# Attention into a gated MoE layer on one core: first batch loaded in fp32 with long rows and cast on the engines, weights behind it, output phase one block late, first MoE tiles by chunk

## The chip, the core and the metric

The kernel runs on one core of a Trainium2 chip. The metric is device microseconds (us) of one execution, of which several are taken. One of the four executions of the kernel before took 997.29 us against 419.54 to 422.00 for the others; it is left out of every ratio (the median of four below still counts it; without it the median is 421.95).

## The reference, cut to what matters

Eight batches of linear attention (8 heads, 576 tokens, head size 64) with a normalised output, then a gated layer over all 4608 tokens of width 512, with 1536 hidden features. Inputs and outputs are fp32.

```python
kv  = einsum('bhsd,bhse->bhde', k, v)          # q, k, v: (8, 8, 576, 64)
o   = einsum('bhsd,bhde->bhse', q, kv)
x   = o / sqrt(mean(o*o, axis=-1) + 1e-6) * g_norm
x   = x.transpose(0, 2, 1, 3).reshape(4608, 512)
ffn = (gelu(x @ w_gate) * (x @ w_val)) @ w_out  # 512 -> 1536 -> 512
out = x + sigmoid(x @ w_res) * ffn
```

## The kernel before

The tokens are cut in blocks of 512: the first 512 tokens of each batch are blocks 0 to 7, and the 64 left over in each batch together make block 8. A block of the MoE layer has 16 slots: twelve feature tiles (eight matmuls of 512 columns each: a gate product `gps` and a value product `vps`) and four output tiles (sixteen matmuls each: `rps`, `fps`). The attention of the next batch is woven into those slots by a fixed plan. Tiles lie in SBUF, the core's memory, here over 128 partitions (its rows) or fewer; results of matmuls lie in the banks of PSUM. Matmuls run on fp16 copies; the DMA that brings in a batch casts it on the way.

```python
    def load_batch(b):                      # (cut: tiles, tokens 512 to 575, q of the rest)
        for j, src in enumerate(main_rows(q, b)):     # rows of 64 fp32 = 256 B
            nc.gpsimd.dma_start(out=q_sb[:, j, :].rearrange("p (h d) -> p h d", h=H), in_=src)
        # ... the same for k and v, four DMAs each, then the rests of k, v and q

    load_batch(0)
    ident32 = consts.tile([P, P], FP32, name="ident32")
    make_identity(nc, ident32)              # POOL: behind the issues of load_batch(0)
    # ... mask, g (broadcast by a DMA to all partitions)
    load_weights()                          # 14 DMAs: gate, value, residual, output
    load_batch(1)                           # behind all weights in the same queue
    # ...
    # one plan of the attention of batch b by slot of the block before it:
    #  0,1: q transposes   2: kv   4-7: outputs   9: norm, scaling   10-15: scalings, transposes of x
    plan = attn_slots(0)                    # batch 0: alone, ahead of block 0
    for s in range(16):
        for f in plan[s]:
            f()
    for blk in range(B + 1):
        # ... load_batch(blk + 2)
        plan = attn_slots(blk + 1)
        for s in range(16):
            if s < NF:
                m_gval(blk, s)              # feature tile s of this block
            else:
                m_out(blk, s - NF)          # output tile of the same block
            for f in plan.get(s, []):
                f()
```

## Time and profile before

| what | value |
|---|---|
| time, median of 4 runs | 421.98 us |
| TensorE busy, of the profiled span of 422.0 us | 358.7 us, 85% |
| packets of the software queue (casting DMAs) | 120928 |
| first MoE matmul | 44.3 us |
| start of block 1 | 105.9 us |
| a block from there on | 39.8 (even batch woven in) or 40.4 us (odd) |

The profile names engines: PE is TensorE (PEld its weight loads), DVE VectorE, ACT ScalarE, POOL GpSimd, SP the engine that issues the plain DMAs. A row of 40 digits gives the busy share of one fortieth of the span in tenths. A line of the order of time has start, duration, engine, source line, operation, what it writes and reads, shapes, and in brackets the idle time ahead of it with what ended it. In a table by stretch, the granted clock is the share of the full TensorE clock that the profile records as granted. Half and full clock, or cold and warm, are names here for two paces of TensorE in the traces: four matmuls of 512 columns took 1.86 to 1.91 us (44.32 and 56.72 in the kernel before) or 1.03 (from 60.12), and a matmul of 128 columns 0.107 or 0.056.

### The profile page before, as it was taken

What the parts mean: (1) busy time and instruction counts of PE and PEld (TensorE: products, weight loads), DVE (VectorE), ACT (ScalarE), POOL (GpSimd) and SP (SyncE); (2) the same over time, 40 slices, a digit from 0 to 9 for tenths busy, and PEclk for the clock granted to TensorE, in tenths of its full rate; (3) what the DMA queues carried; (4) which work ended last, traced back from release to release, by engine and by line L of the source; (5) the groups of instructions that cost most, each with busy time, mean ns of one, the idle gap of its engine ahead of it and who ended that gap; (6) DMA issues with size and microseconds to landing.
All of it is one profiled execution on the core that took longest, in us unless ns stands there. A gap on an engine that the chain in (4) does not pass through costs nothing.

```text
span 422.0 us, 5322 instructions
## 1 busy us (share of the span) xinstructions
PE 358.7 (85%) x2048; PEld 179.5 (43%) x2048; DVE 213.0 (50%) x411; ACT 161.1 (38%) x277; POOL 112.2 (27%) x140
## 2 busy tenths in 40 slices
PE   0052457979998999899899989998999899999994
PEld 0041124524544555445445544554455444444441
DVE  1028111775468447744764586457446853334432
ACT  1024122713463266345434652472347333312320
POOL 6396369940560074009201900000000000000000
PEclk9999998989999999999999999999999999999999
DMA  0999999992790199019911951100200020011013
GB/s 16 100 164 195 207 157 129 142 89 75 68 126 10 66 103 92 26 75 100 69 51 50 137 34 51 50 2 0 75 27 2 0 76 25 1 51 50 0 27 75
DMA packets 127242, 29.45 MB, mean 70 GB/s; under 512 B 114416, under 2 KB 122608, under 8 KB 127216
## 3 DMA queue, kind: packets, MB, share of 16 engines
q0 software_dynamic: 120928, 19.41, 61.5%
q1 hardware_dynamic: 6288, 9.70, 6.7%
q8 instruction: 16, 0.26, 0.3%
q14 instruction: 10, 0.08, 0.1%
HBM read 39.06 MB, written 9.44 MB: 115 GB/s over the span
## 4 chain that ended last, share of the span: by engine, by line
PE 73%; DMA 12%; DVE 8%; POOL 3%; issue 1%; ACT 1%; DVEq 0%; POOLq 0%
PE fps L321 22%; PE gps L299 18%; PE vps L304 18%; PE rps L316 7%; DMA wo<-in_moe_w_out_dram 4%; DMA q_sb<-in_q_dram 4%; PE xtp L264 2%; DMA wv<-in_moe_w_val_dram 2%; POOL v_sb L90 2%; DMA vr<-in_v_dram 2%; PE kvp L174 2%; PE op L193 1%; PE qtp L165 1%; DVE t L250 1%; DVE hid L309 1%
## 5 line engine op out<-in xcount | busy, mean ns | idle before, releaser
L309 DVE TENSOR_TENSOR hid<-ge,vps 128x512 f16<-128x512 f16 x108 | 74.2, 687 | 82.0 <-PE vps L304 81.7
L299 PE MATMUL gps<-xT,wg 128*128 128x512 f16 x432 | 113.1, 385 | 0.7 <-ACT xT L265 0.7
L304 PE MATMUL vps<-xT,wv 128*128 128x512 f16 x432 | 112.1, 382 | 0.0
L321 PE MATMUL fps<-wo,hid 128*128 128x512 f16 x432 | 100.5, 383 | 0.0
L308 ACT ACTIVATE ge<-gps 128x512 f16<-128x512 f32 x108 | 64.8, 600 | 84.0 <-PE gps L299 80.6
L321 PEld LDWEIGHTS <-hid 128*128 128x128 f16 x432 | 42.7, 99 | 52.2 <-issue 2.4
L304 PEld LDWEIGHTS <-wv 128*128 128x128 f16 x432 | 42.6, 99 | 52.3 <-issue 2.3
L86 POOL DMA_DIRECT2D q_sb<-in_q_dram x32 | 28.4, 913 | 108.6 <-PE qtp L165 104.0
L299 PEld LDWEIGHTS <-wg 128*128 128x128 f16 x432 | 40.3, 99 | 38.1 <-issue 2.5
L326 DVE SCALAR_TENSOR_TENSOR pf<-th,fps 128x512 f32<-128x512 f32 x36 | 24.8, 689 | 60.2 <-PE fps L321 60.2
L265 ACT COPY xT<-xtp 128x512 f16<-128x512 f16 x36 | 21.1, 586 | 78.1 <-PE xtp L264 78.1
L165 PE MATMUL qtp<-ident,q_sb 128*128 128x128 f16 x128 | 11.0, 236 | 32.4 <-DVE ident L112 24.6
L316 PE MATMUL rps<-wr,xT 128*128 128x512 f16 x144 | 37.3, 382 | 0.0
L186 DVE TENSOR_REDUCE ss<-sq 128x8 f32<-128x512 f32 x36 | 24.7, 686 | 21.9 <-ACT sq L185 21.9
L166 ACT COPY qT<-qtp 128x1024 f16<-128x1024 f16 x16 | 16.1, 1012 | 43.0 <-PE qtp L165 43.0
L324 ACT ACTIVATE th<-rps 128x512 f32<-128x512 f32 x36 | 21.5, 598 | 27.5 <-PE rps L316 27.5
L90 POOL DMA_DIRECT2D v_sb<-in_v_dram x32 | 28.6, 956 | 9.5 <-DMA q_sb<-in_q_dram 9.5
L88 POOL DMA_DIRECT2D k_sb<-in_k_dram x32 | 28.4, 934 | 9.3 <-DMA wo<-in_moe_w_out_dram 6.2
L264 PE MATMUL xtp<-ident,x 128*128 128x128 f16 x144 | 14.9, 229 | 17.4 <-DVE x L256 17.4
L328 DVE SCALAR_TENSOR_TENSOR osb<-pf,x 128x512 f32<-128x512 f32 x36 | 24.9, 692 | 1.2
L250 DVE TENSOR_TENSOR t<-o,ny 128x512 f16<-128x512 f32 x36 | 24.7, 686 | 0.3
L165 PEld LDWEIGHTS <-q_sb 128*128 128x128 f16 x128 | 9.3, 105 | 36.5 <-DMA q_sb<-in_q_dram 26.7
(49 smaller groups left out, 211.3 us busy)
## 6 DMA issues: line engine op xcount, KB each, us to landing
out_dram<-osb SPq DMA_DIRECT2D x32, 256.0 KB, 2.0
q_sb<-in_q_dram POOLq DMA_DIRECT2D x32, 128.0 KB, 4.3
k_sb<-in_k_dram POOLq DMA_DIRECT2D x32, 128.0 KB, 4.6
v_sb<-in_v_dram POOLq DMA_DIRECT2D x32, 128.0 KB, 4.9
wg<-in_moe_w_gate_dram POOLq DMA_DIRECT2D x6, 256.0 KB, 8.0
wv<-in_moe_w_val_dram POOLq DMA_DIRECT2D x6, 256.0 KB, 8.6
wo<-in_moe_w_out_dram POOLq DMA_DIRECT2D x1, 1536.0 KB, 17.9
out_dram<-osb SPq DMA_DIRECT2D x8, 128.0 KB, 2.3
```

Source lines behind the costliest of these rows:

```text
L86: nc.gpsimd.dma_start(out=q_sb[:, j, :].rearrange("p (h d) -> p h d", h=H), in_=src)
L88: nc.gpsimd.dma_start(out=k_sb[:, j, :].rearrange("p (h d) -> p h d", h=H), in_=src)
L90: nc.gpsimd.dma_start(out=v_sb[:, j, :].rearrange("p (h d) -> p h d", h=H), in_=src)
L250: nc.vector.tensor_tensor(out=t16, in0=s["o"][j].rearrange("p (h d) -> p h d", h=H), in1=s["rinv"][:, j, :, None].to_broadcast([P, H, D]), ...
L299: nc.tensor.matmul(gps, lhsT=wg_c[wi][:, cc, wo_ : wo_ + P], rhs=xT[:, cc, :], start=(cc == 0), stop=(cc == NP - 1))
L304: nc.tensor.matmul(vps, lhsT=wv_c[wi][:, cc, wo_ : wo_ + P], rhs=xT[:, cc, :], start=(cc == 0), stop=(cc == NP - 1))
L308: nc.scalar.activation(out=ge, in_=gps, func=AF.Gelu)
L309: nc.vector.tensor_tensor(out=hids[blk][:, f, :], in0=ge, in1=vps, op=ALU.mult)
L316: nc.tensor.matmul(rps, lhsT=xT_t[blk][:, cc, js], rhs=wr16[:, cc, :], start=(cc == 0), stop=(cc == NP - 1))
L321: nc.tensor.matmul(fps, lhsT=hid[:, f, js], rhs=wo16[:, f, :], start=(f == 0), stop=(f == NF - 1))
L326: nc.vector.scalar_tensor_tensor(out=pf, in0=th, scalar=1.0, in1=fps, op0=ALU.add, op1=ALU.mult)
L328: nc.vector.scalar_tensor_tensor(out=osb, in0=pf, scalar=0.5, in1=x_t[blk][:, j, :], op0=ALU.mult, op1=ALU.add)
```

## The change

The intent is to shorten the start. Its parts:

1. **Load.** Tokens are assigned to partitions so that a partition's tokens are adjacent in memory: four tokens of q on each of 128 partitions (rows of 1024 B), six tokens of k and v on each of 96 partitions (rows of 1536 B). Batch 0 comes as fp32 on SP's queue in halves and is cast on ACT, DVE and POOL; the later batches still use POOL's casting DMA, now with long rows and a 16-bit reorder copy on DVE.
2. **Order of the loads.** The first eight weight pieces are issued by POOL behind its cast, then batch 1, then the rest of the weights.
3. **First MoE tiles by chunk.** Feature tiles 0 and 1 of block 0 are done in four token chunks of 128, so that a chunk can begin when its quarter of x is there.
4. **Output phase one block behind.** A block does its twelve feature tiles and then the four output tiles of the block before it. The last block does two output phases.
5. **Smaller things.** Batch 1's attention starts in slot 7 of block 0; batch 0's norm uses a square root on ACT; the scale by g moves into the copy of the transpose; PSUM is split four and four instead of six and two.

```diff
+    def src_q(b, lo, hi):
+        return q[b, lo:hi, 0:M0, :].rearrange("h (p j) d -> p h (j d)", j=NJ)
+    def src_kv(t, b, lo, hi):
+        return t[b, lo:hi, :, :].rearrange("h (p i) d -> p h (i d)", i=NI)
 ... cut: load_batch for b > 0, with the same rows and POOL's casting DMA ...
-    load_batch(0)
+    for lo in (0, HH):
+        nc.sync.dma_start(out=raw[0, "q"][:, lo : lo + HH, :], in_=src_q(0, lo, lo + HH))
+    for lo in (0, HH):
+        for which, t in (("k", k), ("v", v)):
+            nc.sync.dma_start(out=raw[0, which][:, lo : lo + HH, :], in_=src_kv(t, 0, lo, lo + HH))
 ... cut: identity, mask, constants ...
+    by_token_q(0, 0, HH, nc.scalar.copy)
+    by_token_q(0, HH, H, nc.scalar.copy)
+    a_qT(0, 0)
+    a_qT(0, 1)
+    by_token_k(0, 0, HH, nc.vector.tensor_copy)
+    nc.gpsimd.tensor_copy(out=b16_t[0, "v"][:, 0:HH, :], in_=raw[0, "v"][:, 0:HH, :])
+    a_kv(0, 0, 2)
+    for i in range(4):
+        load_wgv(i)
+    by_token_k(0, HH, H, nc.vector.tensor_copy)
+    nc.vector.tensor_copy(out=b16_t[0, "v"][:, HH:H, :], in_=raw[0, "v"][:, HH:H, :])
+    a_kv(0, 2, 4)
 ... cut: outputs, norm by square root and scaling, chunk by chunk ...
+    nc.vector.tensor_copy(out=grow16, in_=grow[:, None, :].to_broadcast([1, H, D]))
+    gps = pattn.tile([P, C], FP32, tag="at", name="gbp")
+    nc.tensor.matmul(gps, lhsT=ones16, rhs=grow16.rearrange("p h d -> p (h d)"), start=True, stop=True)
+    nc.vector.tensor_copy(out=g16, in_=gps)
 ...
+    def m_gval_first(blk, after):
+        for j in range(NJ):
+            after(j)
+            for f in range(2):
+                m_mm(tiles[2 * f], wg_c, f, blk, j, j + 1)
+                m_mm(tiles[2 * f + 1], wv_c, f, blk, j, j + 1)
 ...
+            first = 7 if blk == 0 else 1
+            plan = {first + i: s for i, s in enumerate(attn_plan(nxt))}
+        if blk == 0:
+            slots = [lambda: m_gval_first(0, lambda j: a_xT(0, j)), None]
+            slots += [lambda f=f: m_gval(0, f) for f in range(2, NF)]
+        else:
+            slots = [lambda f=f: m_gval(blk, f) for f in range(NF)]
+            slots += [lambda j=j: m_out(blk - 1, j) for j in range(NJ)]
+        if blk == B:
+            slots += [lambda j=j: m_out(blk, j) for j in range(NJ)]
 ...
+            if blk == 0 and s == 2:
+                load_batch(1)
+                load_wgv(4)
+                load_wgv(5)
```

## The prediction

> **What bounds the kernel now.** I read the busy slices of the page first, then the table by stretch, then the chain of waits of the start, then the order of time around each hole in TensorE.
>
> ```profile
> PE   0052457979998999899899989998999899999994
> DMA  0999999992790199019911951100200020011013
> q0 software_dynamic: 120928, 19.41, 61.5%
> ```
>
> One slice is 10.55 us. TensorE is full from about the eighth slice on; before that the DMA row is full. The queue row gives 259.5 us of 16 engines for 120928 packets, 34 ns each.
>
> By stretch (busy of PE, weight load, DVE, ACT, POOL; then clock, DMA share, GB/s):
>
> ```profile
> 0.00:44.32 44.32, 8.98 (x69) 6.91 (x69) 12.59 (x37) 9.58 (x15) 28.51 (x40) 1.00 1.22 123
> 44.32:68.60 24.28, 12.60 (x61) 6.20 (x61) 2.07 (x3) 3.72 (x5) 13.22 (x16) 0.95 1.84 164
> 106.79:146.60 39.81, 38.67 (x230) 19.47 (x229) 23.35 (x47) 17.77 (x31) 12.58 (x15) 1.00 0.77 72
> 347.50:382.30 34.80, 34.80 (x163) 15.79 (x162) 13.82 (x21) 9.72 (x17) 0.00 (x0) 1.00 0.09 31
> ```
>
> Two regimes. From 106.8 us on, a block costs 39.8 us with an even batch's attention in it and 40.4 us with an odd one's; block 7, without attention, costs 34.8. A block has 160 MoE matmuls of 512 columns, which go at 0.86 us for four in the chain, 34.5 us. So the steady part is TensorE itself. The first 106 us hold one such block and some 65 us of waiting. The chain of waits and the order of time show what for:
>
> ```profile
> 24.57 1.86 PE L165 MATMUL qtp<-ident,q_sb 128*128 128x128 f16 x16 [24.57 <-DVE ident L112]
> 44.32 1.86 PE L299 MATMUL gps<-xT,wg 128*128 128x512 f16 x4 [0.67 <-ACT xT L265]
> ```
>
> ```profile
> 36.71 17.87 DMA wo<-in_moe_w_out_dram
> 55.75 3.51 POOL v_sb L90 x4
> 59.95 6.73 DMA vr<-in_v_dram
> 68.59 1.34 PE gps L299 x4
> ```
>
> Batch 0 lands by about 27 us. Even the identity is made only at 24 us, as its POOL instructions queue behind the load. The first MoE matmul is at 44.3. Then batch 1, which stands behind all weights in the queue, holds TensorE until 68.6, because its attention is woven into block 0.
>
> [...]a batch is 13824 rows of 256 B and took some 26 us (1.25 to 27.5), 864 rows per engine, 30 ns or 8.5 GB/s per engine; the gate and value weights, rows of 1024 B, 512 per DMA, landed one every 1.34 us (POOL's starts at 38.05, 39.38, 40.75, 42.05, 43.40), 32 rows per engine, 42 ns or 24 GB/s, 390 GB/s over all. [...]The trace's two casts (128 columns 0.23 us, 512 columns 0.43) differ by 0.52 ns per element[...]; the 16-bit rate has no instance here. [...]at 84 us, with POOL issuing DMAs, three small tensor_scalar took 0.77 to 0.84 us, against 0.18 at 36 us. [...]at 44.3 and 56.7 us four matmuls took 1.86 and 1.91 us, from 60 us 1.03 or less.
>
> **The change part by part.**
>
> *Batch 0 load.* 3.4 MB in rows of 1024 B (q) and 1536 B (k, v) on the SP queue, in halves q, q, k, v, k, v, with no DMA cast. At 390 GB/s a q half (0.52 MB) is 1.35 us and a k or v half (0.59 MB) 1.5 us. SP issues its first DMA at 0.74 us; I take 2 us to landing, as the stores show. Landings: 4.1, 5.5, 7.0, 8.5, 10.0, 11.5 us. Against 27.5 before this is 16 us less.
>
> *Casts.* ACT q halves of 1024 elements, about 1.0 us each (the qT copy of 1024 takes 1.01): ready at 6.6, then transposes and qT copies, ready by 10. DVE k half of 1536: 0.16+1536x0.52 ns = 0.96 us. POOL v half: I choose 2 us (its select over 128 columns took 0.29), 10.5 us, TensorE's first half of kv then. DVE casts the second halves by 12.5. Twelve matmuls at cold pace 1.3 us, 13.9; mask 0.69, 14.7.
>
> *Rest of batch 0's attention.* Square from PSUM at 15.8 (0.6), four reductions at 0.69 to 18.6, then on DVE four times a reciprocal (0.15) and a scaling (0.69) with small gaps, 22.1. This replaces the long norm chain of 2.7 us and the eight output evictions. The gelu table load (1.28 in the trace) sits in ACT's gap.
>
> *First MoE tiles by chunk.* The instruction order shows the broadcast of g (cast on DVE behind the last scaling, then a matmul) ahead of the first transpose in TensorE's queue, so no chunk starts before about 22.7: the overlap with the scalings is lost. Then each chunk is serial: transposes 0.4, copy with pointer scale 0.7, 16 matmuls of 128 columns at 0.056 to 0.107, with hand-overs 2.5 us. Four chunks: 32.7 us for feature tiles 0 and 1. Before, they were complete only at about 59 us.
>
> *Block 0.* Ten tiles x 1.73 = 17.3 us. Weights start at 10.5 behind POOL's cast: eight DMAs x 1.35 are in at about 22; batch 1, now long rows, needs 3.4 MB / 390 = 8.7 us plus 512 short rows at 30 ns per engine-row (1 us): in by 33; the last four gate and value pieces by 39, before tile 8 at about 43. So DMA no longer ends any wait. Attention of batch 1 in block 0: 44 small matmuls x 0.056 = 2.5 us, and 0.5 of waits. The last tile ends at 53.0.
>
> *The new hole.* With the output phase a block behind, block 0 has 12 slots while batch 1's attention occupies slots 7 to 20: its outputs, norm and transposes come with nothing beside them. ACT: six passes at 0.5 us, 3.4 us after that tile; last reduction 4.2; norm 12 operations at 0.22, 6.9; four scalings 9.7; transpose and copy 10.9. Block 1 starts at 63.9, and a cold clock costs it 1.7: 65.6 us.
>
> *The remainder.* Blocks 1 to 6 took 240.7 us (39.81+40.40+39.90+40.40+39.80+40.40); 24 instead of 20 matmuls for kv add 4x0.056 each: 242.0. Blocks 7 and 8 took 68.3 (347.5 to 415.8), and block 0's output phase comes on top, 64x0.2158 = 13.8: 82.1. Tail from the last matmul to the end 6.2, as before.
>
> Sum: 65.6+242.0+82.1+6.2 = 395.9, so **396 us**, 6% less. A check: block 1 began at 105.9 before; at 65.6 with 13.8 owed it stands at 79.4, 26.5 less, minus 1.3 for kv.
>
> *PSUM and DVE in the steady part.* Tiles for MoE fall from six to four. The product of tile 10 waits behind norm and two scalings (about 4 us of DVE); its bank is wanted by the output matmuls one tile and a residual group later. The stall I find is about 1.1 us at the first transpose, and the kernel before has that same one (1.14 us idle before its transpose at 130.69, ended by DVE), so I add nothing. The two extra DVE casts per block[...] fit the slack of a tile.
>
> **The rivals.**
> 1. *A PSUM or DVE bound in steady blocks.* Against: DVE is 23 to 25 us busy of 40[...]. For: four banks leave one tile of slack[...]. 1 to 2.5 us per block for six blocks: 402 to 411.
> 2. *The hole is larger or smaller.* The norm's small operations at the 0.84 seen under POOL's issues would add 2 us; the chain starting earlier would take 3 off. 393 to 399.
> 3. *The load does not reach 390 GB/s, or POOL's cast is slow.* [...]4 us of POOL cast gives 2 more and delays the weights. 397 to 400.
> 4. *The load was hidden anyway.* Then the time would stay at 422. Against: the holes of 7.6 us at 48 to 55 and the 24.57 at the start are TensorE's own, and nothing else fills them.
> 5. *Startup quicker* (chunks at 2 us, hole 8): 388 to 391.
>
> **Range and chances.** The saving of 26 us comes from landings that are shown, and the debts (hole, chunks) from durations that are shown. The main risk is rival 1, upward. Range 387 to 408. Faster by over 2% means below 413.6: 0.95; within 2%: 0.04; slower: 0.01.
>
> **What would show each step.** Batch 0's last half landing at 11 to 13 us; the first transposes of q near 7 us; the last scaling at 20 to 24 and the g matmul between it and the first x transpose; tile 2 at 30 to 34; no DMA among TensorE's long waits after that; an idle of 8 to 11 us on TensorE between 50 and 67 us, ended by ACT's copy of xT; blocks of 40.0 and 40.6 us from then on; the software queue's share falling from 61.5% to some 24% (seven batches at 9.7 us, weights 27 us, of 396). The prediction is wrong if steady blocks take over 41 us, if TensorE waits for weights in block 0, or if the hole is absent.

## The result and the profile after

The kernel after takes 404.08 us (median of four runs, 403.59 to 404.58), the kernel before 421.98. The ratio is 0.959, with a 95% interval from 0.955 to 0.964. A ratio in this document compares the fast runs of two kernels in the same rounds, so it is not quite the ratio of the medians quoted. 404.08 lies inside the predicted range of 387 to 408, and 8 us above its centre of 396.

The same rows of the page, now of the kernel after (one digit is 10.07 us):

```profile
PE   2337993999999999999999999999999999999994
DMA  8999978091119011901190119011001100200113
q0 software_dynamic: 30896, 17.70, 32.1%
```

TensorE is now full from the eighth slice as before, but it is already nearly full in slices 5 and 6. A single digit 3 follows them: that is the hole which the prediction described. Packets of the software queue fell to a quarter. Its share, 32.1%, is more than the 24% predicted: 0.321 x 402.8 us x 16 engines / 30896 is 67 ns per packet. The two numbers are not of one kind: the 24% was worked out from landing times, while the page adds up the durations of packets, and these overlap (in e6 below the same row shows 120.4% between 2 and 17 us).

By stretch (length, then busy time and count of PE, weight load, DVE, ACT, POOL; granted clock, DMA share, GB/s), the kernel after:

```profile
28.10:40.55 12.45, 9.35 (x82) 8.64 (x82) 1.30 (x2) 3.73 (x6) 3.98 (x5) 1.00 1.45 197
...
63.70:73.04 9.34, 3.38 (x25) 2.03 (x24) 8.80 (x24) 4.32 (x8) 0.00 (x0) 0.70 0.48 56
113.40:153.90 40.50, 39.76 (x249) 20.45 (x248) 25.82 (x50) 18.51 (x31) 3.11 (x4) 1.00 0.40 71
```

The first is the chunk loop, the second the hole before block 1, with PE busy for 3.4 of 9.3 us. Block 2 (the third) takes 40.5 us: the steady part is as it was.

The order of time of the start in the kernel after, DVE, POOL and ACT (casts of batch 0):

```profile
10.39 0.96 DVE L108 CAST k<-kf 96x1536 f16<-96x1536 f32 x1 [7.54 <-DMA kf<-in_k_dram]
...
12.84 1.46 POOL L386 CAST v<-vf 96x1536 f16<-96x1536 f32 x1 [11.53 <-DMA vf<-in_v_dram]
...
14.99 0.96 DVE L108 CAST k<-kf 96x1536 f16<-96x1536 f32 x1 [3.65 <-DMA kf<-in_k_dram]
...
16.39 0.96 DVE L391 CAST v<-vf 96x1536 f16<-96x1536 f32 x1 [0.44 <-DMA vf<-in_v_dram]
```

Each cast begins when its half lands. The k and v halves land at 10.4, 12.8, 15.0 and 16.4 us; 7.0, 8.5, 10.0 and 11.5 were predicted.

TensorE in the order of time, kernel after, around the chunk loop:

```profile
27.57 0.60 PE L403 MATMUL gbp<-grow,ones 1*128 1x512 f16 x1 [6.08 <-DVE grow L401]
28.10 0.61 PE L259 MATMUL xtp<-ident,t 128*128 128x128 f16 x4
...
32.55 0.58 PE L283 MATMUL gps<-xT,wg 128*128 128x128 f16 x4 [0.78 <-ACT xT L260]
...
35.62 0.58 PE L283 MATMUL gps<-xT,wg 128*128 128x128 f16 x4 [0.78 <-ACT xT L260]
...
40.35 1.91 PE L283 MATMUL gps<-xT,wg 128*128 128x512 f16 x4
...
43.68 1.03 PE L283 MATMUL gps<-xT,wg 128*128 128x512 f16 x4
```

The broadcast of g stands ahead of the first transpose of x, as predicted. A chunk takes 3.07 us (32.55 to 35.62), of which 0.78 is an idle wait for ACT's copy. Four matmuls of 128 columns start 0.43 us apart from the next four, 0.107 each, for all four chunks, where e7 below has 0.056 for the same matmuls. This document calls that pace half clock; it is read from the durations, since the column of the granted clock shows 1.00 for this stretch. Tile 2 (40.35) is still at half clock; only tile 3 (43.68) has the full pace, 0.864 us from one group of four matmuls of 512 columns to the next.

The hole, kernel after, DVE first, then TensorE:

```profile
62.97 3.50 DVE L173 TENSOR_REDUCE ss<-sq 128x8 f32<-128x512 f32 x5
66.50 0.18 DVE L219 TENSOR_SCALAR nm<-ss 128x40 f32<-128x40 f32 x1
...
69.11 2.48 DVE L247 TENSOR_TENSOR t<-op,ny 128x512 f16<-128x512 f32 x4
```

```profile
69.86 3.00 PE L259 MATMUL xtp<-ident,t 128*128 128x128 f16 x20 [5.74 <-DVE t L247]
73.04 1.64 PE L283 MATMUL gps<-xT,wg 128*128 128x512 f16 x4 [0.17 <-ACT xT L260]
```

From the end of tile 11 (61.7 us) to block 1 (73.0) it is reductions, twelve small norm operations and scalings in series, with nothing for TensorE but a few matmuls of the outputs and the transposes.

### The profile page after: what moved, and what is told of

Its sections match the earlier page's. It is cut to its first block, busy times and chain, and to the rows that moved or that the text cites. A ratio compares the mean times of both kernels' runs of the same rounds, so it can differ in the third digit from the quotient of the medians.

```text
span 402.8 us, 5424 instructions
## 1 busy us (share of the span) xinstructions
PE 362.3 (90%) x2129; PEld 185.9 (46%) x2129; DVE 216.4 (54%) x411; ACT 154.6 (38%) x252; POOL 36.6 (9%) x50
## 3 DMA queue, kind: packets, MB, share of 16 engines
q0 software_dynamic: 30896, 17.70, 32.1%
## 4 chain that ended last, share of the span: by engine, by line
PE 87%; DMA 5%; DVE 3%; POOL 2%; ACT 2%; issue 1%; SPq 0%; DVEq 0%; ACTq 0%
PE gps L283 24%; PE vps L283 24%; PE fps L322 23%; PE rps L317 8%; DMA vf<-in_v_dram 3%; PE kvp L158 2%; DMA qr<-in_q_dram 2%; PE xtp L259 2%; PE qtp L147 2%; PE op L179 1%; DVE t L247 1%; ACT xT L260 1%; POOL wg L122 1%; POOL wv L123 1%; DVE ss L173 1%
## 5 line engine op out<-in xcount | busy, mean ns | idle before, releaser
L283 PE MATMUL gps<-xT,wg 128*128 128x512 f16 (+1 forms) x456 | 115.3, 378 | 3.3 <-ACT xT L260 2.5
L283 PE MATMUL vps<-xT,wv 128*128 128x512 f16 (+1 forms) x456 | 114.7, 376 | 0.0
L260 ACT ACTIVATE xT<-xtp,gcol 128x512 f16<-128x512 f16 x36 | 23.2, 686 | 42.2 <-PE xtp L259 42.2
L172 ACT ACTIVATE sq<-op 128x512 f32<-128x512 f32 x32 | 19.0, 597 | 22.6 <-PE op L179 22.0
L329 DVE SCALAR_TENSOR_TENSOR osb<-pf,t 128x512 f32<-128x512 f32 x36 | 24.9, 692 | 1.2
L259 PE MATMUL xtp<-ident,t 128*128 128x128 f16 x144 | 15.1, 243 | 10.0 <-DVE t L247 10.0
L158 PE MATMUL kvp<-v,k 96*128 96x128 f16 x192 | 14.6, 230 | 7.1 <-POOL v L386 5.4
L317 PEld LDWEIGHTS <-xT 128*128 128x128 f16 x144 | 13.4, 98 | 13.5
L259 PEld LDWEIGHTS <-t 128*128 128x128 f16 x144 | 10.3, 107 | 17.7 <-DVE t L247 15.1
L247 DVE TENSOR_TENSOR t<-op,ny 128x512 f16<-128x512 f32 x28 | 17.9, 684 | 0.3
## 6 DMA issues: line engine op xcount, KB each, us to landing
qraw<-in_q_dram POOLq DMA_DIRECT2D x7, 512.0 KB, 10.9
wo<-in_moe_w_out_dram POOLq DMA_DIRECT2D x1, 1536.0 KB, 18.6
kf<-in_k_dram SPq DMA_DIRECT2D x2, 576.0 KB, 10.4
```

Source lines behind the costliest of these rows:

```text
L158: nc.tensor.matmul(ps[:, pr, :], lhsT=k16[:, i, pr * P : (pr + 1) * P], rhs=v16[:, 2 * pr : 2 * pr + 2, i * D : (i + 1) * D], start=(i == ...
L247: nc.vector.tensor_tensor(out=t_t[blk][:, jj, :].rearrange("p (h d) -> p h d", h=H), in0=s["o"][j].rearrange("p (h d) -> p h d", h=H), in1 ...
L259: nc.tensor.transpose(ps[:, cc, :], t_t[blk][:, jj, cc * P : (cc + 1) * P], ident)
L260: nc.scalar.activation(out=xT_t[blk][:, :, jj * P : (jj + 1) * P], in_=ps, func=AF.Copy, scale=gcol)
L283: nc.tensor.matmul(ps[:, j0 * P : j1 * P], lhsT=w[:, cc, :], rhs=xT_t[blk][:, cc, j0 * P : j1 * P], start=(cc == 0), stop=(cc == NP - 1),)
L317: nc.tensor.matmul(rps, lhsT=xT_t[blk][:, cc, js], rhs=wr16[:, cc, :], start=(cc == 0), stop=(cc == NP - 1))
```

## The experiments

The open question is where 8 us of the expected gain went, and what the debts which the prediction already named (hole, chunks, deferral) really cost. All runs are correct. Times are medians of four runs; the ratio is to the kernel before (421.24, 422.42 and 421.21 us on three chips).

| run | edit to the kernel after | us | ratio | 95% interval |
|---|---|---|---|---|
| (after) | | 404.08 | 0.959 | 0.955 to 0.964 |
| e1_start2 | batch 1's attention from slot 2 | 400.32 | 0.952 | 0.949 to 0.955 |
| e2_nochunk | first tiles whole | 400.08 | 0.950 | 0.948 to 0.953 |
| e3_glater | broadcast of g behind the chunks | 403.68 | 0.959 | 0.956 to 0.961 |
| e4_sameblock | output phase in its own block | 402.16 | 0.955 | 0.953 to 0.958 |
| e5_all | these four together | 388.64 | 0.921 | 0.917 to 0.925 |
| e6_pool0 | batch 0 by POOL's casting DMA | 401.35 | 0.951 | 0.948 to 0.955 |
| e7_warm | filler matmuls in the chunk loop | 401.00 | 0.950 | 0.947 to 0.954 |
| e8_kv128 | k, v of batch 0 over 128 partitions | 402.09 | 0.953 | 0.949 to 0.957 |
| e9_all_pool | e5_all and e6_pool0 | 385.28 | 0.916 | 0.910 to 0.921 |
| e10_all_kv128 | e5_all and e8_kv128 | 385.77 | 0.917 | 0.913 to 0.921 |

The intervals of some single edits touch that of the kernel after, so for those the traces carry the argument more than the times. The traces have a spread of their own: the kernel after, e1, e2, e4 and e7 have the same program up to the first transpose of x, yet it starts at 28.10, 27.10, 28.46, 27.30 and 28.41 us, because batch 0 lands at different times. Each kernel was profiled once, so a gain of 1 us at the start of a single profile means nothing by itself.

### e1: batch 1's attention earlier

```diff
-            first = 7 if blk == 0 else 1
+            first = 2 if blk == 0 else 1
-            if blk == 0 and s == 2:
+            if blk == 0 and s == 0:
```

> The changed kernel with one edit: batch 1's attention starts at slot 2 of block 0 instead of slot 7 (and its load is issued in the program before that, the queue order is unchanged). Theory: the 11.2 us hole on TensorE before block 1 (61.85 to 73.04 in the profile after) exists only because slots 12 to 20 have no MoE tile beside them; started at slot 2 only the last scalings, transposes and copies are left behind tile 11, a hole of 3.5 to 4 us, and no cold restart. Then the time falls by 7 to 9 us, to about 396 us. Rival: batch 1's rows land too late for slot 2 (slot 7 was chosen for the load), DVE waits for them with the products of tiles 3 and on behind it, and the time is 402 to 406 us.

Measured: 400.32 us, 3.8 less where 7 to 9 were expected. The rival falls: batch 1's q was there when DVE came to it. But the hole shrank only to about 6 us. DVE and TensorE in the order of time, e1:

```profile
60.81 0.69 DVE L274 TENSOR_TENSOR hid<-ge,vps 128x512 f16<-128x512 f16 x1 [0.26 <-PE vps L283]
61.41 0.18 DVE L219 TENSOR_SCALAR nm<-ss 128x40 f32<-128x40 f32 x1
```

```profile
64.70 0.40 PE L259 MATMUL xtp<-ident,t 128*128 128x128 f16 x4 [2.27 <-DVE t L247]
...
68.47 1.86 PE L283 MATMUL gps<-xT,wg 128*128 128x512 f16 x4 [0.18 <-ACT xT L260]
```

In this trace DVE runs its instructions in the order of the program. The norm stands behind the product of tile 10 (`hid`, 60.81), so it cannot begin before 61.4, while TensorE does its last product of the block (it ends at about 62.4). The earlier slots took the reductions out of the hole, but not the norm and the scalings. Starting the attention earlier closes the hole only if something else fills TensorE while DVE normalises. Of the 4.6 us by which block 1 starts earlier here (68.47 against 73.04), 1.0 is the quicker landing in this profile and not the edit.

### e2: the first tiles whole

```diff
-            slots = [lambda: m_gval_first(0, lambda j: a_xT(0, j)), None]
+            def whole():
+                for j in range(NJ):
+                    a_xT(0, j)
+                m_gval(0, 0)
+                m_gval(0, 1)
+            slots = [whole, None]
```

> The changed kernel without the tiles by chunk: four transposes one behind the other, then feature tiles 0 and 1 at full width. Theory: the serial chunk loop (12.45 us, matmuls at 0.107 us) keeps TensorE at half clock and also makes tile 2 run cold; at full width the last xT copy ends near 31.6 us,[...] tile 2 ends at about 38.7 us instead of 43.85. Time falls by 4 to 6 us, to 398 to 400 us. Rival: the chunks do save time as intended (work starts before the last xT); then without them the time rises by 1 to 3 us.

Measured: 400.08 us, 4.0 less; the theory expected 398 to 400. TensorE in the order of time, e2:

```profile
31.57 1.86 PE L283 MATMUL gps<-xT,wg 128*128 128x512 f16 x4 [1.23 <-ACT xT L260]
...
34.59 1.03 PE L283 MATMUL gps<-xT,wg 128*128 128x512 f16 x4
```

```profile
67.42 1.86 PE L283 MATMUL gps<-xT,wg 128*128 128x512 f16 x4 [0.18 <-ACT xT L260]
...
72.14 1.03 PE L283 MATMUL vps<-xT,wv 128*128 128x512 f16 x4
```

Tile 0 starts 2.1 us later than the first chunk did (31.57 against 29.49), but the clock is full from 34.6, and tile 2 is finished at 38.05 instead of 43.68. Chunking is a loss here: with the broadcast of g in the way it overlaps nothing, and it adds four hand-overs. Block 1 starts 5.6 us earlier (67.42 against 73.04), yet the time is only 4.0 less. The second fence shows why: behind the hole the clock took 2.1 us extra to come back (three products took 4.72 us, from 67.42 to 72.14, in place of 2.59 at 0.864 each), against 0.6 in the kernel after.

### e3: the broadcast of g out of the way

```diff
     # cut: the cast of g on DVE, the matmul and the copy become g_bcast(), a step of slot 0 behind the chunk loop
+            plan.setdefault(0, []).append(g_bcast)
```

> The changed kernel with the broadcast of g (cast, matmul, copy) moved behind the first two feature tiles. Theory: the matmul of g in TensorE's queue, which waits for DVE behind the last scaling, holds the first chunk from about 24.6 us (first scaling done at 24.47) to 28.1; without it the first transpose is at 24.6 and tile 2 starts about 3.5 us earlier, less up to 1.5 us that the g matmul now waits behind DVE's first products. Time falls by 2 to 3.5 us, to 400.5 to 402 us. Rival: the chunk loop is paced by something else (weights, DVE) and starts no earlier: 404 us, same.

Measured: 403.68 us, which is no measurable difference to the kernel after, and above the range expected. TensorE in the order of time, e3:

```profile
23.58 0.61 PE L259 MATMUL xtp<-ident,t 128*128 128x128 f16 x4 [3.05 <-DVE t L247]
...
37.37 0.58 PE L404 MATMUL gbp<-grow,ones 1*128 1x512 f16 x1 [1.31 <-DVE grow L402]
37.88 1.89 PE L283 MATMUL gps<-xT,wg 128*128 128x512 f16 x4
```

The first transpose starts 4.5 us earlier, some 1 us of it because batch 0's scalings happened to be ready earlier in this profile. Of the 4.5, tile 2 keeps 2.5 (37.88 against 40.35): behind the loop the broadcast still costs 1.8, a wait of 1.31 for DVE and 0.5 for the matmul, and the loop itself is as cold and serial as before. Block 1 also starts 2.5 us earlier (70.52 against 73.04), but the clock's return there costs 2.3 us (three products in 4.89 less 2.59) against 0.6 in the kernel after, which takes 1.7 of it. What reached the end is too little to measure.

### e4: the output phase in its own block

```diff
-            slots += [lambda j=j: m_out(blk - 1, j) for j in range(NJ)]
+            slots += [lambda j=j: m_out(blk, j) for j in range(NJ)]
-        if blk == B:
-            slots += [lambda j=j: m_out(blk, j) for j in range(NJ)]
     # and the same four slots in block 0
```

> The changed kernel with the output phase in its own block again (undoes that part of the change). Theory: the deferral gains nothing in steady blocks (they cost 39.6 to 40.5 us, as before), so steady blocks stay within 0.3 us; in block 0 the outputs fill slots 12 to 15 beside batch 1's attention, but its norm is queued on DVE behind the last output, so a hole of some 8 us stays: 3 us less in all, about 401 us. Rival A: the deferral hides a wait in every block, and undoing it costs 0.5 to 1 us per block, 404 to 409 us. Rival B: the output weights are not there in block 0 and TensorE waits for them.

Measured: 402.16 us, 1.9 less (3 expected). Block 1 starts at 83.39 with block 0's output done, against 73.04 and 13.8 us of output phase owed, 86.8, in the kernel after: 3.4 earlier, of which 1.5 had been won before tile 3 already (42.17 against 43.68), by the landing and a quicker clock and not by the edit. Steady blocks did not change, so the deferral buys nothing there. But filling block 0 with its own output phase did not close the hole, because the attention plan starts at slot 7 and still ends behind slot 16. TensorE in the order of time, e4:

```profile
80.21 3.00 PE L259 MATMUL xtp<-ident,t 128*128 128x128 f16 x20 [4.72 <-DVE t L247]
83.39 1.87 PE L283 MATMUL gps<-xT,wg 128*128 128x512 f16 x4 [0.18 <-ACT xT L260]
```

### e5: the four together

> The changed kernel with four edits: batch 1's attention from slot 2, no chunks, g broadcast behind tiles 0 and 1 (its cast early on ACT), output phase in its own block. Theory: the hole before block 1 closes, as both the attention starts early and the outputs stand beside its end, and with it the cold restart goes; tiles 0 and 1 start at about 28.5 us and run at full width. Block 1 then starts at 71 us with its outputs done; 240.4 for blocks 1 to 6, 69.0 for 7 and 8, 5.7 tail: span 386, time 386 to 390 us. Rival: the parts overlap (each wins the same wait): 396 to 398 us; or the output weights (landed at 54.5 us after) stop TensorE in block 0 at slot 12, which comes at about 57 us: up to 3 us more.

Measured: 388.64 us, as expected, 15.4 us less than the kernel after. The four gains taken alone add up to 10.1 (3.8, 4.0, 0.4, 1.9). (One thing is more than the four: in e3 the cast of g stayed on DVE, here it is on ACT.) TensorE in the order of time, e5:

```profile
29.18 1.86 PE L283 MATMUL gps<-xT,wg 128*128 128x512 f16 x4 [0.78 <-DMA qr<-in_q_dram]
...
69.61 2.75 PE L322 MATMUL fps<-wo,hid 128*128 128x512 f16 x12
72.20 1.03 PE L283 MATMUL gps<-xT,wg 128*128 128x512 f16 x4
```

Block 1 starts at 72.20 with block 0's output done, warm, right behind a matmul. The kernel after stood at 73.04 with a restart of 0.6 and 13.8 us of output phase owed, which makes 87.4: 15.2 us later, and 15.4 is what the time shows. Of the 15.2, 7.1 are won ahead of tile 3 (36.59 against 43.68), where e2 and e3 alone won 5.6 and 2.5. The other 8.1 come from the hole and the restart, where e1 and e4 alone, without what their profiles had won ahead of tile 3, moved block 1 by 3.6 and 1.9. So it is e1 and e4 that need each other: an early start moves the norm to where the output phase can cover it, and the output phase is there to cover only if it is not deferred. The order of time fits that, but the two without e2 and e3 were not run. (The bracket of the first line names a DMA. The last transpose ended 0.78 us before, the same wait as in the chunk loop's lines, so I read it as ACT's copy; e10's profile names ACT's copy at this place.)

### e6: batch 0 by POOL's casting DMA, rows still long

```diff
-        nc.sync.dma_start(out=raw[0, "q"][:, lo : lo + HH, :], in_=src_q(0, lo, lo + HH))   # fp32 tile
+        nc.gpsimd.dma_start(out=raw[0, "q"][:, lo : lo + HH, :], in_=src_q(0, lo, lo + HH)) # fp16 tile
     # the same for k and v, in the order q q k v k v; the two casts of v are gone
```

> The changed kernel with one part undone: batch 0 is loaded by POOL with the cast in the DMA, as batches 1 to 7 are (same long rows, same halves, order q q k v k v), so there is no fp32 in SBUF, no cast of v, and the weights follow in POOL's queue. Theory: fp32 rows over 96 partitions are slow to write (102 ns per 1536 B row per engine at the start, against 76 ns for the same rows with the cast in the later batches), so the POOL load lands v at 13.5 us instead of 16.4 and needs no cast: mask at 15.2 instead of 18.9 us, time 3 to 4 us less, about 400.5 us. Rival: the fp32 load is what makes the start fast; with POOL's issue and the cast DMA it starts later and lands at 16 us or after: time equal or up to 4 us more.

Measured: 401.35 us, 2.7 less, a little short of the 3 to 4 expected. So the fp32 landing is not what made the load fast: the last half lands earlier without it. Against the kernel before, which casts in the DMA too, what is left is long rows and 6 DMAs for batch 0's main part in place of 14. DVE and TensorE in the order of time, e6:

```profile
9.63 0.56 DVE L108 COPY k<-kr 96x1536 f16<-96x1536 f16 x1 [6.79 <-DMA kr<-in_k_dram]
...
14.06 1.44 PE L158 MATMUL kvp<-v,k 96*128 96x128 f16 x12 [1.53 <-DMA v<-in_v_dram]
```

ACT's second copy of q starts 1 us later than in the kernel after (7.14 against 6.12), but the last v half is there at 14.06 instead of 16.39, although the same fp32 bytes are read in the same rows.

### e7: filler in the chunk loop

```diff
+            dm = pattn.tile([P, NP, P], FP32, tag="at", name="dm")
+            for i in range(10):          # results never read
+                nc.tensor.matmul(dm[:, 0, :], lhsT=ident, rhs=ident, start=True, stop=True)
```

> The changed kernel with ten matmuls of 128 columns without use after each chunk's transposes (results are right, their tile is never read), which fill TensorE's wait for the xT copy. Theory: the chunk loop runs at 0.107 us per matmul because its gaps keep the clock at half; without gaps the clock is full from the second or third chunk on: loop 10 to 10.5 us instead of 12.45 and tile 2 at full clock (1.73 instead of 3.3): 3 to 4 us less, 400 to 401 us. Rival: 128-column matmuls with a fresh weight load each go at 0.107 us here whatever the clock; then the loop grows by the fill, 0 to 3 us, and the time is 404 to 407 us.

Measured: 401.00 us, 3.1 less, by adding forty useless matmuls. TensorE in the order of time, e7:

```profile
29.88 0.63 PE L283 MATMUL gps<-xT,wg 128*128 128x128 f16 x4
...
32.99 0.38 PE L283 MATMUL gps<-xT,wg 128*128 128x128 f16 x4
...
38.17 1.02 PE L283 MATMUL gps<-xT,wg 128*128 128x512 f16 x4
```

From the second chunk on the clock is full (0.38 for four in place of 0.58), and tile 2 is warm. Nothing else was changed, so the pause of 0.78 us per chunk is what kept the kernel after at half clock until tile 3 at 43.68. (Whether the pause alone or also the transposes beside it keep the pace low is not tested apart: the filler adds to both.) The rival (weight loads set the pace) falls.

### e8: k and v of batch 0 over 128 partitions

```diff
-        raw[0, which] = t[0:KP] ...                       # 96 partitions, rows of 1536 B
+        raw[0, which] = t ...[:, 0 : NP * 9 * D] ...      # 128 partitions, rows of 2304 B
     # a pair of heads lies on 128 partitions, a head on 64; kv by 72 matmuls with 64 rows
```

> The changed kernel with k and v of batch 0 laid over 128 partitions instead of 96 (two heads side by side, 64 partitions each, nine tokens a partition, rows of 2304 B instead of 1536, same bytes; kv then takes 72 matmuls of 64 columns instead of 24 of 128). Theory: k and v land late[...]; over 128 they land at q's rate, 1.76 us per half, the last at 13.1 instead of 16.4 us. The extra small matmuls take 1 us back: time about 2 us less, 402 us. Rival: it is not the partitions (rows, HBM or the queue): the last half lands at 16 us or later and the time is 404 to 406.

Measured: 402.09 us, 2.0 less, as expected. The halves land at 9.25, 10.76, 12.16 and 13.56 us. The last half lands at 15.2 to 16.9 us in the seven profiles with the old layout, and at 12.6 in e10, which has the new one too, so this is more than the spread. The rate of the DMAs between 2 and 17 us (each number is 0.375 us), first the kernel after, then e8:

```profile
GB/s 145 208 360 388 382 366 385 370 284 255 246 283 315 242 201 238 258 270 250 238 225 258 250 250 254 217 254 225 262 246 266 213 168 136 74 33 30 46 122 164
```

```profile
GB/s 82 180 360 390 385 391 382 360 352 342 375 369 369 406 387 375 399 399 430 418 406 399 406 387 131 49 49 25 25 25 0 7 31 90 184 199 190 194 199 191
```

In both, q (128 partitions) moves at some 380 GB/s. With k and v over 96 partitions the rate drops to about 250; over 128 it stays between 340 and 430. The rows of e8 are also longer, but that is not the reason: q has the shortest rows of all (1024 B), lies over 128 partitions and moves at 380.

### e9 and e10: the best of both

```diff
     # e9: all of e5 and e6; e10: all of e5 and e8
```

> Everything of e5_all (388.64 us), and batch 0 loaded by POOL's casting DMA as in e6_pool0, which alone gave 2.7 us. Theory (the start is one serial chain up to the first MoE matmul, and the landing of batch 0 is its first link): the two gains add, about 385.5 us, 384.5 to 387; the first gate product at about 26 us against 29.2. Rival (with the holes gone, block 0 is paced by what lands behind batch 0 in the same queue: weights, batch 1, output weights): the gain is lost in a DMA wait inside block 0, 388 to 389.

> Everything of e5_all (388.64 us), and k and v of batch 0 laid over 128 partitions as in e8_kv128, still fp32 on the SP queue with casts on the engines. Theory[...]: 386 to 387 us, about 2 less, the first gate product at about 27 us. Rival (the saving is eaten by the clock or by a later wait): 388 to 389. If e9_all_pool and this one agree within 1 us, the cast on the engines itself costs next to nothing[...].

Measured: 385.28 and 385.77 us, ratios 0.916 and 0.917 to the kernel before, both faster than the kernel after. The medians are 3.4 and 2.9 us below that of e5 (388.64), but on another chip, and the intervals of the ratios overlap with e5's (0.917 to 0.925): by the times alone the step from e5 is likely, not shown. The traces show it. From 25.5 to 68.3 us TensorE of e9 is busy for 42.6 of 42.8 us, so no wait for a DMA eats the gain. TensorE in the order of time, e9, then e10:

```profile
25.51 1.87 PE L283 MATMUL gps<-xT,wg 128*128 128x512 f16 x4 [0.78 <-DMA qr<-in_q_dram]
...
68.26 1.03 PE L283 MATMUL gps<-xT,wg 128*128 128x512 f16 x4
```

```profile
35.49 0.62 PE L147 MATMUL qtp<-ident,q 128*128 128x128 f16 x8 [1.00 <-DVE q L102]
```

The first MoE matmul comes 3.7 us earlier than in e5 (25.51 against 29.18), and block 1 3.9 us earlier. The two ways of loading end within 0.5 us of each other, which is no difference that these runs resolve. They get there differently: e10 starts its first product 0.6 us before e9 (24.90) and loses 1.0 us at 35.49, where TensorE waits for DVE's copy of batch 1's q, and DVE for the DMA that brings it (e5 has the same wait, 0.76 us). So of e10's rival, a later wait that eats the gain, there is at most 0.24 us.

## Why the prediction was right, and where its terms were off

The mechanism was right (a start that waits, a steady part that does not move, a debt in the form of a hole), and two terms of its sum were too small: the landing of k and v, and the chunks with tile 2. The predicted sum was 395.9 us of span; the profiled execution has 402.8. The difference of 6.9 us by steps of the prediction (starts from the order of time; the restart is the time above 0.864 us per group of four matmuls; the 1.7 predicted for it was the author's estimate, and agrees with the kernel before, where two groups from 44.32 took 3.57 us and two from 60.12 took 1.89):

| step | predicted | measured | difference |
|---|---|---|---|
| first transpose of x starts | 22.7 | 28.10 | +5.4 |
| four chunks | 10.0 | 12.25 | +2.25 |
| tile 2 | 1.73 | 3.33 | +1.6 |
| tiles 3 to 11 with batch 1's attention | 18.6 | 18.0 | -0.6 |
| the hole | 10.9 | 11.35 | +0.45 |
| restart of the clock at block 1 | 1.7 | 0.6 | -1.1 |
| blocks 1 to 6 | 242.0 | 240.4 | -1.6 |
| blocks 7 and 8 | 82.1 | 83.1 | +1.0 |
| tail | 6.2 | 5.7 | -0.5 |

**What held.** TensorE is the bound of the steady part and did not move: 40.5 us per block with an odd batch woven in and 39.6 to 39.7 with an even one (predicted 40.6 and 40.0). The rival of a PSUM or DVE bound, whose size was the author's estimate, did not occur. The 16-bit reorder copies took 0.69 us for 2048 elements per partition and 0.95 for 3072 (0.26 ns per element by their difference, against 0.52 for the casts from fp32 in the kernel before). The hole has the size and the cause that were worked out from single durations, and e1, e4 and e5 show how it hangs on the plan. After the start no DMA is among TensorE's long waits. The first broadcast of g, with its lost overlap, was read correctly from the instruction order. One reading of the kernel before was loose: of the "some 65 us of waiting" in the first 106 us, TensorE's own rows show 50 of idle time (it is busy for 56.8 of 106.8); the rest is the attention of two batches and matmuls at half clock.

**The signs it named.** The first transposes of q (5.65 and 7.22 us), the g matmul ahead of the first transpose of x, the block times and the absence of DMA waits came as said. The last half (16.39 against 11 to 13), the last scaling (26.50 against 20 to 24) and tile 2 (40.35 against 30 to 34) came late. The hole came with its length, but not as one idle of 8 to 11 us ended by ACT: TensorE's longest wait in it is 5.74 us, ended by DVE's scaling, and transposes stretched over 3 us follow.

**Mis-sized: the landing of k and v.** "A k or v half (0.59 MB) 1.5 us" at 390 GB/s took about 2.4 us (0.59 MB at 250 GB/s); the last cast started at 16.39 instead of 11.5, which is 4.9 of the 5.4 us. The prediction took its rate from loads onto 128 partitions and applied it to 96. Spreading over 128 partitions (e8) and halving the bytes written into the same 96 partitions (e6) both bring the last half 2.3 to 2.8 us earlier, and the mean spacing of the four halves falls from 2.0 us ((16.39 - 10.39) / 3) to 1.4 (e8) and 1.5 (e6). That these two very different edits end alike speaks for the side that writes (e6 also changes the queue, e8 does not); that is argued, not shown.

**Mis-sized: chunks and tile 2.** The prediction gave a chunk 2.5 us with matmuls at "0.056 to 0.107", and tile 2 the warm 1.73. All four chunks ran at 0.107, and tile 2 paid the warm-up. Together they cost 3.85 us more than priced. Pauses of 0.78 us in every 3.07 were enough to keep the clock low. e7 shows it by filling the pause.

**Where the expected gain went.** Of the 6.9 us of span, 5.4 lie ahead of the first transpose, nearly all of it the load of k and v, and 3.85 in the chunks and tile 2, mostly by the clock, less 2.35 that the other terms gave back. The rest of the 8 us above the centre is that the sum was one of span while the metric lies above the span (404.58 against 402.8 us in the profiled execution, which is 0.5 above the median); the prediction overlooked that. The hole, the chunks and the deferral it had counted as debts, correctly; e5 shows that they were avoidable, and worth 15.4 us together with the cold chunks. That 404.08 lies in the range is in part luck: the prediction had priced a slow load at 397 to 400, and the place where the result fell, 402 to 411, stood for the PSUM and DVE bound, which did not occur.

**What stays open.** A cold restart cost between 0.5 us (e7) and 2.3 us (e3), with the same kind of hole before it. It hides part of the gains of e2, e3, e6 and e8. These runs show the spread, not the cause.

## What to carry to other kernels

Price a load by the number of partitions it lands on (here about 250 GB/s over 96, 340 to 430 over 128) as well as by the length of its rows (8.5 GB/s per DMA engine with 256 B, 24 with 1024 B in the kernel before), and price a fill phase at the slow clock when TensorE pauses regularly, as it did here for 0.78 us in every 3.07. When a serial chain on DVE has to be hidden, look first for matmul work that is already allowed to run beside it (here the block's own output phase), before pushing that work a block later. Edits that each close a part of one hole can be worth more together than in sum, as here (15.4 us against 10.1): try them together before dropping one that gains little alone.

## What these runs show of the hardware

- Over 96 partitions the loads of k and v moved at about 250 GB/s with fp32 rows of 1536 B (kernel after), against 340 to 430 over 128 partitions with rows of 2304 B (e8).
- Pauses of 0.78 us in every 3.07 us kept the clock at half for all four chunks (0.107 us per matmul of 128 columns, kernel after); with the pause filled it was full from the second chunk on (0.056, e7).
- The cost of coming back after a hole of 6 to 11 us was 0.5, 0.6, 0.9, 1.1, 1.8, 2.1, 2.1 and 2.3 us in eight profiles (e7, kernel after, e1, e4, e6, e2, e8, e3). For an edit worth 2 to 4 us that variation is nearly as large as the effect.
- POOL's casting DMA filled 96 partitions with fp16 out of fp32 rows of 1536 B at one half of 0.59 MB per 1.5 us (e6), faster than the plain copy of the same rows into fp32 (2.0 us between halves, kernel after).
- The loads of e8 moved at 340 to 430 GB/s for 8 us, with one core at work.
- A cast of 1536 fp32 elements per partition to fp16 took 1.46 us on POOL and 0.96 on DVE (kernel after).
